# Half of the weight ring and half of the gated rows moved by 32 bytes: hash attention followed by a SwiGLU block

## The chip, the cores and the metric

The kernel runs on one core of a Trainium2 chip. The metric is the time on the device of one launch, in microseconds (us), median of the runs. A second number, the span, is the time from the first to the last instruction in one execution that was taken by the hardware profiler.

## The reference

Two blocks follow one another, all in float32.

```python
# attention with a hash mask: B, H, S, D = 4, 8, 768, 64; proj is 64 x 6
q_bucket = sum(((q @ proj) > 0) * powers);  k_bucket = the same of k
scores = where(q_bucket == k_bucket, q @ k.T / sqrt(D), -1e9)
attn_out = softmax(scores) @ v
# SwiGLU block: x is 3072 x 512, w_gate and w_val 512 x 1536, w_out 1536 x 512
x = attn_out as (B * S, H * D)
g = x @ w_gate
out = (silu(g) * (x @ w_val)) @ w_out
```

## The kernel before

**Two stages.** `attention` runs first, for 16 pairs of heads. Beside it the weights of the second block are turned into pieces of 128 x 3 x 512 float32 numbers and kept in DRAM (`ram`). A piece has three parts: high, low and the difference of the two. Rows of `x` are split into the same three parts. A product is then made of two sums of matmuls, one over the high and low parts (`a`) and one over the differences (`n`), and combined on the way out of PSUM. `gated_block` is the second stage, and the only one that the diff touches.

**Work of the second stage.** The 3072 tokens are three blocks of 1024. For each block there are 12 tasks U, numbered on through the blocks (n = 0 to 35), one for each 128 columns of the hidden dimension, and 4 tasks D (12 in all), each for three U. The list `order` (lines 219 to 225) writes the sequence out: U 0 to 3, D 0, U 4 to 6, D 1, and so on.

- A U makes two units, one for the gate and one for the value. A unit uses one ring place as the weights (the stationary operand) of 24 matmuls of 128 x 512: 16 into `a`, then 8 into `n` (`up`, lines 672 to 693). The moving operand is `xparts`: four tiles, j = 0 to 3, each with two halves of 512 tokens and three parts. For each half, `a` goes through j, and for each j through parts 0 and 1; `n` goes through j with part 2. ScalarE and VectorE then make the gated row tile `hid` from it, 128 x 3 x 1024 numbers (lines 709 to 726).
- A D goes through eight chunks of 128 tokens. Each chunk has nine matmuls (lines 738 to 754): for j = 0 to 2 the parts 0 and 1, then for j = 0 to 2 part 2. Here the weights are 128 columns of `hid` number 3 D + j, and the moving operand is a ring place with 512 columns. In the last D of a block the first four chunks begin with j = 0 and 1 alone. The sums go to `o` (lines 756 to 775), and after the fourth D of a block to DRAM.

**The weight ring.** The ring has six places. The first three, numbered 0 to 2, are in the pool `ringp`, made before the attention; the other three, 3 to 5, are in `late_ring`, made when the attention's buffers are given back. The list `wanted` (lines 226 to 231) holds the pieces in their order of use, and piece number i of it goes to place i mod 6 (`bring`, lines 234 to 244):

```python
pool = ringp[i % sum(RINGS) >= RINGS[0]]
held[what, n] = t = pool.tile([P, 3, PIECE], FP32R, tag="ring", name="ring")
nc.gpsimd.dma_start(t.bitcast(FP32), ram[at].bitcast(FP32))
```

Each unit asks for one more piece when its matmuls are written down, and each D for three. The loads go through the queue of GpSimd (POOL). The rows `hid` have four places, taken in turn.

**Where `xparts` lies** (`x_home`, lines 250 to 261). In block 0 all four tiles are in the pool `xparts`. In block 1, j = 0 and 1 are in the two buffers of the pool `stagep`, and j = 2 and 3 in `xparts`. In block 2, j = 0 and 1 are in `xparts`, and 2 and 3 in `stagep`.

**Addresses.** Pools lie one after another along each partition, in the order in which the code makes them (lines 69 to 76, then those of the stage), and a tile's room is rounded up to 32 bytes. All tile sizes of the second stage are multiples of 2048 bytes, as are the steps between the parts of a tile; the blocks of weights inside a part are 512 bytes apart. So whether a matmul's operand lies at a multiple of 64 bytes or 32 bytes past one is decided by the start of its tile. In the built program before, `stagep` begins at byte 28800 (offset 0 in 64), `xparts` at 53664 (offset 32), `ringp` at 105888 (32), `late_ring` at 124320 (32), `gatep` at 142752 (32), `hidp` at 159136 (32) and `outp` at 208288 (32).

Of the kernel before, what the change touches and what calls it, by code (L numbers as in the profile page):

```python
# [8 lines left out]
FP32 = mybir.dt.float32  # L9
FP32R = mybir.dt.float32r  # L10
# [9 lines left out]
def kernel(  # L20
# [24 lines left out]
    P = 128  # L45
# [12 lines left out]
    WB = 2 * PIECE  # L58
# [41 lines left out]
    n = 0  # L100
# [550 lines left out]


    def gated_block(scope):
        ringp.append(scope.enter_context(tc.tile_pool(name="late_ring", bufs=RINGS[1])))
        gatep = scope.enter_context(tc.tile_pool(name="gatep", bufs=2))
        hidp = scope.enter_context(tc.tile_pool(name="hidp", bufs=4))
        outp = scope.enter_context(tc.tile_pool(name="outp", bufs=1))
        homes.append(outp)
        pp = scope.enter_context(tc.tile_pool(name="pp", bufs=4, space=PSUM))
# [4 lines left out]
        hids = {}  # L664
# [33 lines left out]
        def atoms_of(kind, n):  # L698
            if kind == "U":
                b = n // NF  # L700
                hid = hids[n] = hidp.tile([P, 3, WB], FP32R, tag="hid", name="hid")
                h, l, d = (hid[:, i] for i in range(3))
                gate, val = (gatep.tile([P, WB], FP32, tag=name, name=name) for name in "gv")
                ops = {}
# [108 lines left out]
        for kind, n in order:  # L813
# [12 lines left out]
            for at, atom in enumerate(atoms_of(kind, n)):  # L826
                tail = atom()
                finish(tails)
                if tail:
                    tails.append(tail)  # L830
                if changing and kind == "U" and f >= NF - 2 and at:
                    splits.pop(0)()
                if changing and kind == "D" and f == NF // NQ - 1:
                    if at == 0:
                        more = [split_x(b + 1, pr) for pr in range(NP // 2, NP)]
                        for x in more:
                            x.pop(0)()
                    if at in (7, 10):
                        for x in more:
                            x.pop(0)()  # L840
                count[0] += 1
                if left and count[0] in (6, 14):
                    left.append(left.pop(0)())
                    left[:] = [f for f in left if f]
                for _ in range(((1, 2, 2, 2) if kind == "U" else (1, 2, 2) + (1,) * 9)[at]):
                    step = next(mine, None)
                    if step:
                        step()

    with ExitStack() as scope:  # L850
        gated_block(scope)
# [32 lines left out]
```

## Time and profile before

| what | us |
|---|---|
| median of 3 runs (923.06 to 925.82) | 923.29 |
| the profiled execution's own time | 927.82 |
| its span | 926.0 |
| busy in the span: TensorE (PE) / VectorE (DVE) / ScalarE (ACT) | 912.7 / 666.4 / 456.2 |
| start of the first matmul of the second stage | 325.43 |
| first matmul of blocks 1 and 2 | 522.12 / 721.66 |
| end of the last matmul | 921.36 |
| busy with the 1152 `a`, 576 `n` and 864 `o` matmuls | 277.0 / 144.3 / 198.7 |

The granted clock of TensorE is 0.998 of full speed over the span. In the page, a line such as "L670" is a line of the kernel. All matmuls of the second stage are written by one helper, `mm`, and so have the line 670; they are told apart by the tile that they write. PEld is the loading of weights into TensorE, which goes on beside matmuls. A matmul is recorded with its start and with an end that is modelled, and it is still in the pipeline when the next begins; so the time that a row of matmuls takes is read from starts. In the rows of a timeline the columns are the start and the length in us, the engine, the line, the operation with its tiles and shapes, and the number of instructions that are merged. In the waits they are the total in us, the number of times and the longest. In the view of one line, the three numbers are the shortest, median and longest duration in ns.

### The profile page before, as it was taken

What the parts mean: (1) busy time and instruction counts of PE and PEld (TensorE: products, weight loads), DVE (VectorE), ACT (ScalarE), POOL (GpSimd) and SP (SyncE); (2) the same over time, 40 slices, a digit from 0 to 9 for tenths busy, and PEclk for the clock granted to TensorE, in tenths of its full rate; (3) what the DMA queues carried; (4) which work ended last, traced back from release to release, by engine and by line L of the source; (5) the groups of instructions that cost most, each with busy time, mean ns of one, the idle gap of its engine ahead of it and who ended that gap; (6) DMA issues with size and microseconds to landing.
All of it is one profiled execution on the core that took longest, in us unless ns stands there. A gap on an engine that the chain in (4) does not pass through costs nothing.

```text
span 926.0 us, 12980 instructions
## 1 busy us (share of the span) xinstructions
PE 912.7 (99%) x4789; PEld 638.9 (69%) x4789; DVE 666.4 (72%) x768; ACT 456.2 (49%) x814; POOL 91.6 (10%) x182
## 2 busy tenths in 40 slices
PE   8999989999999999999999999999999999999997
PEld 3444544444444478888888788888887888888886
DVE  4889989889989858779786756464658754474746
ACT  6889868888888654452414133331313233313220
POOL 2011100001101111000100000101010100001000
PEclk9999999999999999999999999999999999999999
DMA  7678787767886599685756563434444642526232
GB/s 171 136 185 205 201 207 172 166 180 200 242 213 206 179 384 318 229 284 206 292 187 243 207 226 103 175 133 170 137 145 151 234 147 103 187 69 208 99 136 92
DMA packets 145296, 174.28 MB, mean 188 GB/s; under 512 B 106481, under 2 KB 114897, under 8 KB 145233
## 3 DMA queue, kind: packets, MB, share of 16 engines
q0 software_dynamic: 22528, 116.14, 36.0%
q1 hardware_dynamic: 121904, 57.12, 24.3%
q8 instruction: 38, 0.62, 0.3%
q10 hardware_dynamic: 800, 0.20, 0.1%
q14 instruction: 26, 0.20, 0.1%
HBM read 133.17 MB, written 39.42 MB: 186 GB/s over the span
## 4 chain that ended last, share of the span: by engine, by line
PE 95%; DVE 2%; DMA 1%; SPq 1%; issue 0%; ACT 0%; DVEq 0%; ACTq 0%; POOLq 0%
PE a L670 29%; PE o L670 19%; PE sc L504 16%; PE n L670 14%; PE av L518 14%; PE sum L557 1%; PE hps L436 1%; SPq L337 1%; DMA kraw<-in_k_dram 0%; DVE hid L725 0%; DVE v L715 0%; DVE hid L723 0%; DVE v L719 0%; DMA qb<-qb 0%; DMA proj<-in_proj_dram 0%
## 5 line engine op out<-in xcount | busy, mean ns | idle before, releaser
L670 PE MATMUL a<-xparts,ring 128*128 128x512 f32 x1152 | 277.0, 392 | 0.6 <-ACT row L560 0.6
L670 PEld LDWEIGHTS a<-xparts,ring 128*128 128x128 f32 x1152 | 216.2, 188 | 50.2 <-ACT row L560 1.3
L670 PE MATMUL o<-ring,hid 128*128 128x512 f32 x864 | 198.7, 390 | 1.1 <-DVE hid L725 1.1
L670 PEld LDWEIGHTS o<-ring,hid 128*128 128x128 f32 x864 | 161.9, 188 | 36.0 <-DVE hid L725 2.4
L507 ACT ACTIVATE A<-sc 128x384 f32<-128x384 f32 x384 | 157.3, 492 | 12.6 <-PE sc L504 12.6
L504 PE MATMUL sc<-qT,kT 64*128 64x384 f32 x768 | 158.9, 491 | 0.0
L670 PE MATMUL n<-xparts,ring 128*128 128x512 f32 x576 | 144.3, 393 | 0.0
L518 PE MATMUL av<-A,vraw 128*64 128x386 f32 (+1 forms) x768 | 127.7, 488 | 0.0
L670 PEld LDWEIGHTS n<-xparts,ring 128*128 128x128 f32 x576 | 108.1, 188 | 24.3
L715 DVE TENSOR_TENSOR v<-v,n 128x1024 f32<-128x1024 f32 x36 | 44.0, 1221 | 104.0 <-PE n L670 103.4
L244 POOL DMA_DIRECT2D ring<-ram x108 | 56.9, 529 | 506.9 <-PE n L670 334.9
L504 PEld LDWEIGHTS sc<-qT,kT 64*128 64x128 f32 x768 | 69.2, 189 | 51.3 <-issue 50.3
L518 PEld LDWEIGHTS av<-A,vraw 128*64 128x64 f32 x768 | 53.7, 136 | 73.3 <-issue 61.6
L709 ACT ACTIVATE g<-a 128x1024 f32<-128x1024 f32 x36 | 37.0, 1026 | 134.0 <-PE a L670 127.8
L720 ACT ACTIVATE hid<-v 128x1024 fp32r<-128x1024 f32 x36 | 38.2, 1061 | 115.9 <-DVE v L719 112.9
L717 ACT ACTIVATE g<-g 128x1024 f32<-128x1024 f32 x36 | 38.2, 1061 | 84.7 <-DVE g L715 84.7
L772 DVE TENSOR_TENSOR o<-o 128x512 f32<-128x512 f32 x92 | 63.0, 687 | 20.6 <-ACT o L766 18.2
L504 PE MATMUL sc<-qb,kb 64*128 64x384 bf16 x384 | 65.4, 325 | 3.4 <-DMA qb<-qb 2.9
L715 DVE TENSOR_TENSOR g<-g,n 128x1024 f32<-128x1024 f32 x36 | 43.8, 1216 | 34.2 <-PE n L670 34.2
L539 DVE SCALAR_TENSOR_TENSOR both<-A 128x1536 f32<-128x1536 f32 x32 | 55.9, 1748 | 13.6 <-ACT A L507 13.0
L543 DVE TENSOR_TENSOR both<-both,A 128x1536 f32<-128x1536 f32 x32 | 56.3, 1759 | 3.3
L723 DVE SCALAR_TENSOR_TENSOR hid<-hid,v 128x1024 fp32r<-128x1024 f32 x36 | 44.0, 1223 | 19.2 <-ACT hid L720 19.1
(76 smaller groups left out, 696.9 us busy)
## 6 DMA issues: line engine op xcount, KB each, us to landing
ring<-ram POOLq DMA_DIRECT2D x108, 768.0 KB, 5.1
ram<-stage POOLq DMA_DIRECT2D x23, 768.0 KB, 5.7
ram<-stage SPq DMA_DIRECT2D x13, 768.0 KB
qraw<-in_q_dram SPq DMA_DIRECT2D x64, 96.0 KB
vraw<-in_v_dram SPq DMA_DIRECT2D x16, 384.0 KB
out_dram<-o SPq DMA_DIRECT2D x24, 256.0 KB
kraw<-in_k_dram SPq DMA_DIRECT2D x62, 96.0 KB
r<-sums SPq DMA_DIRECT2D x30, 192.0 KB
```

Source lines behind the costliest of these rows:

```text
L244: nc.gpsimd.dma_start(t.bitcast(FP32), ram[at].bitcast(FP32))
L504: nc.tensor.matmul(sc[h], x["k", n][rows, ks], x["q", n][rows, qs], start=start, stop=not start)
L507: nc.scalar.activation(weights(u)[:, h, 0:HQ], sc[h], AF.Exp, scale=SCALE * (OFF / 2 if n == 0 else 1.0))
L518: nc.tensor.matmul(ps[h * D : (h + 1) * D, 0:width], raws["v", n][:, h, c, :], a[:, h, 0:width], start=c == 0, stop=c == NCH - 1)
L539: nc.vector.scalar_tensor_tensor(out=t, in0=first, scalar=S * EPS / P / 2, in1=now, op0=ALU.add, op1=ALU.add)
L543: nc.vector.tensor_tensor(t, t, now, op=ALU.add)
L670: nc.tensor.matmul(ps, w, x, start=start, stop=stop)
L715: nc.vector.tensor_tensor(two(z), two(z), n_, op=ALU.subtract)
L717: nc.scalar.activation(z, z, AF.Silu)
L720: nc.scalar.activation(h, val, AF.Copy, scale=TOWARD / STEP)
L723: nc.vector.scalar_tensor_tensor(out=l, in0=h.bitcast(FP32), scalar=-STEP, in1=val, op0=ALU.mult, op1=ALU.add)
L772: nc.vector.tensor_tensor(accs[c], accs[c], t[:, 1], op=ALU.subtract)
```

## The change

Three small tiles of 32 bytes per partition, which nothing reads or writes, are laid between the pools of the second stage, and the pool of the gated rows is made into two of two buffers each. In the built program `late_ring` begins at byte 124352 (offset 0 in 64), `gatep` at 142816 (32), the first two gated rows at 159200 (32), the other two at 183808 (0), and `outp` at 208384 (0). Gated rows with an even n take the buffers of the first pool and those with an odd n the buffers of the second; a buffer is used again after four, as before. The number of instructions and their order on each engine are the same.

```diff
     def gated_block(scope):
+        def shift(name):
+            scope.enter_context(tc.tile_pool(name=name, bufs=1)).tile([P, 8], FP32, tag=name, name=name)
+
+        shift("shift_ring")
         ringp.append(scope.enter_context(tc.tile_pool(name="late_ring", bufs=RINGS[1])))
+        shift("shift_gate")
         gatep = scope.enter_context(tc.tile_pool(name="gatep", bufs=2))
-        hidp = scope.enter_context(tc.tile_pool(name="hidp", bufs=4))
+        hidp = [scope.enter_context(tc.tile_pool(name="hidp", bufs=2))]
+        shift("shift_hid")
+        hidp.append(scope.enter_context(tc.tile_pool(name="more_hid", bufs=2)))
         outp = scope.enter_context(tc.tile_pool(name="outp", bufs=1))
...
-                hid = hids[n] = hidp.tile([P, 3, WB], FP32R, tag="hid", name="hid")
+                hid = hids[n] = hidp[n % 2].tile([P, 3, WB], FP32R, tag="hid", name="hid")
```

## The prediction

> **What bounds the kernel now.** I read the page first: busy times and the chain that ended last.
>
> ```profile
> PE 912.7 (99%) x4789; PEld 638.9 (69%) x4789; DVE 666.4 (72%) x768; ACT 456.2 (49%) x814; POOL 91.6 (10%) x182
> ...
> PE 95%; DVE 2%; DMA 1%; SPq 1%; issue 0%; ACT 0%; DVEq 0%; ACTq 0%; POOLq 0%
> PE a L670 29%; PE o L670 19%; PE sc L504 16%; PE n L670 14%; PE av L518 14%; PE sum L557 1%; PE hps L436 1%; SPq L337 1%; DMA kraw<-in_k_dram 0%; DVE hid L725 0%; DVE v L715 0%; DVE hid L723 0%; DVE v L719 0%; DMA qb<-qb 0%; DMA proj<-in_proj_dram 0%
> ```
>
> TensorE carries 95% of the chain, and 62% of the span is the matmuls of line 670, the gated block, which alone uses the buffers that move. Next, the waits of PE from 318 us to the end:
>
> ```profile
> PE o L670 <- DVE hid L725: 1.1, 3, 0.4
> PE a L670 <- ACT row L560: 0.6, 1, 0.6
> ```
>
> PE waits 1.7 us in 600. So the stage lasts as long as its 2592 matmuls, and the question is the time from one matmul's start to the next, the pitch. A matmul's own duration overlaps the next one, so I read starts, in the timeline of PE. Two units of the first token block, then two of the second (a unit is 16 `a` and 8 `n` matmuls on one ring place):
>
> ```profile
> 347.34 3.79 PE L670 MATMUL a<-xparts,ring 128*128 128x512 f32 x16
> 350.97 1.98 PE L670 MATMUL n<-xparts,ring 128*128 128x512 f32 x8
> 352.78 3.79 PE L670 MATMUL a<-xparts,ring 128*128 128x512 f32 x16
> ...
> 527.69 3.88 PE L670 MATMUL a<-xparts,ring 128*128 128x512 f32 x16
> 531.40 2.02 PE L670 MATMUL n<-xparts,ring 128*128 128x512 f32 x8
> 533.25 3.88 PE L670 MATMUL a<-xparts,ring 128*128 128x512 f32 x16
> ```
>
> From `a` to the next `a`: 352.78 - 347.34 = 5.44 us in block 0, 226.7 ns a matmul; 533.25 - 527.69 = 5.56 us in block 1, 231.7 ns. Same instructions, no idle time in either. The down projection, from the chain in order of time, one row in each block:
>
> ```profile
> 369.26 16.32 PE o L670 x72
> ...
> 566.82 16.32 PE o L670 x72
> ...
> 766.35 16.32 PE o L670 x72
> ```
>
> 16.32/72 = 226.7 ns in all three blocks. What differs between the two kinds of unit is where `xparts` lies. In block 0 all four home tiles are in the `xparts` pool, 32 bytes past a multiple of 64, as every ring place is. In blocks 1 and 2 two of the four are in the `stage` buffers, at a multiple of 64. Starts of single matmuls in the unit at 632.7 us show it: in `n` the pitches are 235, 235, 230, 227, then 234, 235, 231, 227 ns, for tiles j = 0 to 3, of which 0 and 1 are those in `stage`. In block 2 `stage` holds 2 and 3, and the slow ones swap with it. So a pair of matmuls whose moving operand lies at offset 0 while the weights lie at 32 loses 7.5 + 8.3 ns, and the next one 4.1. By the grouped line 670 in one unit of each kind:
>
> ```profile
> L670 PE MATMUL a<-xparts,ring x16: 389/389/389, 352.8 to 356.2; 128*128 128x512 f32 x16
> ...
> L670 PE MATMUL a<-xparts,ring x17: 389/395/397, 632.7 to 638.3; 128*128 128x512 f32 x17
> ```
>
> The excess over 226.67 ns, summed over starts, is 0.04 us in U of block 0, 3.04 in block 1, 3.02 in block 2, 0.13 in all D. That is 6.06 us for 576 matmuls at offset 0, 10.5 ns each with what spills into neighbours.
>
> **The Trainium skill.** "TensorE: Matmul & The Clock Gate", Step-by-step: what each phase is for, says PE has two independent SBUF read ports, so that loading the next weights takes nothing from the running matmul. The trace disagrees twice: 226.7 ns is above the 215.7 ns that the same page gives for back-to-back matmuls of 512 columns (Wait — 56ns, not 53.3ns?), and the pitch depends on where an operand lies. "SBUF — State Buffer", Operand start alignment, calls any multiple of the element size legal, and says its runs timed nothing. The same page (Door 1) tells of 16-byte lines; all operands here start on such a line, so it prices nothing.
>
> **The change part by part.** Order and count of instructions on every engine stay as they are; addresses move. Offsets in 64 bytes, before to after: ring places 0 to 2 stay at 32; places 3 to 5 go 32 to 0; gated rows of even n stay at 32, of odd n go 32 to 0; `g` and `v` stay at 32; `o` goes 32 to 0; `xparts` stays. I call a matmul mixed when its moving operand and its weights differ in this offset. Before: 576 mixed, 6.06 us.
>
> *U, block 0*: of 24 units 10 take their weights from places 3 to 5, now at 0, against `xparts` at 32: 240 mixed. Long runs cost less each than pairs; the second run of four in a slow unit alternates 7.5 and 5.7 ns, the first 7.5, 8.3, 5.0, 8.3, so 7 ns: 240 x 7 = 1.7 us.
>
> *U, blocks 1 and 2*: the 28 units with early places stay as they are. The 20 with late places have weights at 0: the tiles in `stage` now match, the other two are mixed. 12 of 24 before, 12 after: nothing, if mixed costs the same both ways round.
>
> *D* (moving: ring; weights: gated rows): before, none mixed. After, walking the ring order (places 2,3,4; 5,0,1; 2,3,4; 3,4,5 in each block) against odd and even n, just one of the three j in each D is mixed: 24 of 72 matmuls, in each chunk one pair (v = 0, 1) and one single (v = 2). Pair 19.9 ns as measured; single 7.5 + 4.1 = 11.6, an estimate from the same row: 8 x 31.5 = 0.25 us, times 12 = 3.0 us.
>
> *VectorE and ScalarE*: same kinds before and after; 1024-wide operations on `xparts` in `stage` take 1217 to 1226 ns as on the others. Even 10 ns on each would hide under PE: DVE works 384 us of the stage's 596. Uncovered, the last PE tail has two such operations: 0.02 us.
>
> *Waits*: the wait for the xT store that line 720 had at n = 0 (3.0 us, ACT idle, PE not) goes to n = 1, when the store has long landed. One PE wait in the first D moves two matmuls back. Ring loads keep their waits; they land in 5.1 us and are asked for five units (27 us) ahead. Nothing.
>
> Sum: 1.7 + 3.0 = 4.7 us for 528 more mixed matmuls; at 6.6 or 10.5 ns each it is 3.5 or 5.5. The profiled execution is 927.82 us (926.0 span, 1.8 around it), 4.5 above the median 923.29; its matmul pitches are repeated to the nanosecond in every unit, so I add the difference to the median.
>
> **Unknown prices.** Three pairings never occur before: moving 32 on weights 0, 0 on 0, and equal in 64 but 64 apart in 128 (all matching matmuls above are equal in 512). Below, streaming alone is 512/2.4 GHz = 213.3 ns, so a matmul could gain at most 13.3; above, the slowest seen is 236, a loss of 9. I take each by its offset in 64, since 0 against 32 is the only contrast that the trace has.
>
> **Rivals.**
> *Only the moving offset counts.* A moving operand at 0 is slow whatever the weights. For it: every slow matmul has one. Then U stays, and D has 576 such matmuls (ring places 3 to 5), in pairs and fours: at 19.9 ns a pair and 43 a four, 5.3 us. It can't be told by time from my sum; together they put the change at 4.7 to 5.3, and I take 4.9. Should the weights being loaded for the next matmul decide, D has 569 mixed and the sum is 6.9.
> *Finer than 64.* If only operands equal in 128 bytes run at 226.7, another 816 are slow: at about 7 ns in long runs the total is 14.6 against 6.06, +8.6 us, 931.9.
> *One direction only.* Weights at 32 under moving 0 is slow, the reverse free. Then mixed falls to 336 in U and rises by 216 in D: 5.8 against 6.06, 923.0; by next weights +1.2. Nothing in the trace speaks against it.
> *Faster: the new distance of 64 is better than 0.* 226.7 is 13.3 above streaming, so equal addresses may themselves collide. 816 matmuls get this distance. It decides when each gains over 4.7/816 = 5.8 ns; at 11 ns (down to the page's 215.7) -9.0 + 4.7 = -4.3, 919.0. Against it: all pitches of the trace but two, just after a start of PE, are 226 or more.
> *It does nothing*: `stage` is slow for its place, not its offset, and the time stays. Against it: `stage` ends at 53376 and the first fast `xparts` tile begins at 53664.
>
> **Numbers.** Mixed or moving offset counts (4.7 to 6.9): 0.62. Finer than 64: 0.10. One direction: 0.13. Nothing: 0.05. Faster: 0.10. The likeliest is 923.3 + 4.9 = 928.2, its own range 926.5 to 930.5. The range for 8 in 10 goes from 922.5 (one direction, nothing) to 932.5 (finer than 64) and leaves out the faster rival. About 0.3% (2.8 us) is what a measurement can tell; slower 0.72, same 0.18, faster 0.10.
>
> **What would show it.** Units of block 0 on late places at 5.6 us beside 5.44 on early ones; D at 16.57 us for 72; units of blocks 1 and 2 at 5.56. Moving only: block 0 all 5.44, D at 16.7 to 16.8. One direction: block 0 all 5.44 and late units of blocks 1 and 2 too. Wrong altogether: a pitch below 226, or new idle time of PE ahead of line 670.

## The result and the profile after

| | before | after |
|---|---|---|
| median of 3 runs, us | 923.29 (923.06 to 925.82) | 929.09 (928.66 to 931.45) |
| the profiled execution's own time / its span | 927.82 / 926.0 | 931.45 / 929.6 |
| second stage: start of its first matmul to end of its last | 325.43 to 921.36: 595.92 | 323.11 to 924.98: 601.88 |

The changed kernel is slower: the ratio is 1.0067, with a 95% interval of 1.0046 to 1.0087, and the medians are 5.8 us apart. The spans of the two profiled executions are only 3.6 us apart, because the first stage, which the change does not touch, took 2.3 us more in the execution before. There PE waited 2.9 us for a transfer of `qb`, against 2.1 after, and TensorE's granted clock was at half from 131.4 to 134.8 us, where it was full after. The second stage is 5.96 us longer, and that is the number that answers to the medians.

The groups of the page after, with the lines of TensorE (busy us, mean ns of one, then idle time before):

```profile
L677 PE MATMUL a<-xparts,ring 128*128 128x512 f32 x1152 | 278.1, 393 | 0.6 <-ACT row L560 0.6
...
L677 PE MATMUL o<-ring,hid 128*128 128x512 f32 x864 | 203.3, 395 | 0.7 <-DVE hid L732 0.7
...
L677 PE MATMUL n<-xparts,ring 128*128 128x512 f32 x576 | 144.8, 393 | 0.0
```

Line 670 is now 677. Against 277.0, 198.7 and 144.3 us before, most of the new time is in `o`, the matmuls of D. It is not idle time. The waits of PE in the second stage:

```profile
PE o L677 <- DVE hid L732: 0.7, 3, 0.3
PE a L677 <- ACT row L560: 0.6, 1, 0.6
```

They were 1.1 and 0.6 us before. The matmuls themselves follow one another more slowly. In the timeline of PE in block 0, the first two rows are units on early ring places, the next three on late ones, which the change moved (rows of `n` left out):

```profile
328.68 3.79 PE L677 MATMUL a<-xparts,ring 128*128 128x512 f32 x16
...
334.12 3.79 PE L677 MATMUL a<-xparts,ring 128*128 128x512 f32 x16
...
339.57 3.89 PE L677 MATMUL a<-xparts,ring 128*128 128x512 f32 x16
...
345.16 3.90 PE L677 MATMUL a<-xparts,ring 128*128 128x512 f32 x16
...
350.76 3.90 PE L677 MATMUL a<-xparts,ring 128*128 128x512 f32 x16
```

From start to start the units on early places take 5.44 and 5.45 us, as before, and those on late places 5.59 and 5.60. A D took 16.32 us before, in each of the nine that have no wait of PE in them. After, in the chain in order of time (start, us, what):

```profile
367.41 16.75 PE o L677 x72
...
417.29 16.68 PE o L677 x72
...
567.54 16.75 PE o L677 x72
```

Summed over the starts of single matmuls, the excess over 226.67 ns is now 12.49 us against 6.23 (both with D): U of block 0 has 1.68 (before 0.04), U of blocks 1 and 2 together 6.10 (6.06), D 4.71 (0.13). The place of the loss is the one that was forecast. What makes a matmul slow turned out to be another rule. The prediction also named a pitch below 226 ns as a sign of being wrong; there are 27 single ones of 224 or 225 ns after, each with slow pitches next to it, and no row that is faster than before.

### The profile page after: what moved, and what is told of

It is laid out like the page before. It is cut to its first block, busy times and chain, and to the rows that moved or that the text cites. A ratio compares the mean times of both kernels' runs of the same rounds, so it can differ in the third digit from the quotient of the medians.

```text
span 929.6 us, 12980 instructions
## 1 busy us (share of the span) xinstructions
PE 917.8 (99%) x4789; PEld 638.4 (69%) x4789; DVE 666.8 (72%) x768; ACT 456.7 (49%) x814; POOL 91.6 (10%) x182
## 4 chain that ended last, share of the span: by engine, by line
PE 91%; DVE 3%; SPq 3%; DMA 2%; ACT 1%; issue 1%; DVEq 0%; ACTq 0%
PE a L677 29%; PE o L677 20%; PE n L677 14%; PE sc L504 14%; PE av L518 11%; SPq L337 2%; PE sum L557 1%; PE hps L436 1%; DMA kraw<-in_k_dram 0%; PE idle L367 0%; DVE hid L732 0%; DVE hid L730 0%; DVE v L722 0%; DVE v L726 0%; DMA r<-sums 0%
## 5 line engine op out<-in xcount | busy, mean ns | idle before, releaser
L677 PE MATMUL o<-ring,hid 128*128 128x512 f32 x864 | 203.3, 395 | 0.7 <-DVE hid L732 0.7
L775 DVE SCALAR_TENSOR_TENSOR o<-o 128x512 f32<-128x512 f32 x72 | 49.4, 687 | 12.9 <-PE o L677 12.7
```

The lines of the kernel that those rows point to most:

```text
L677: nc.tensor.matmul(ps, w, x, start=start, stop=stop)
L775: nc.vector.scalar_tensor_tensor(out=accs[c], in0=t[:, 0], scalar=STEP + 1, in1=accs[c], op0=ALU.mult, op1=ALU.add)
```

## The experiments

In the following, the distance of a matmul is the address of its moving operand minus that of its weights, in bytes along the partition. Where a number under 256 is given for it, that is the remainder of a division by 256, which turned out to be what counts: 224 means 32 bytes short of a multiple. A matmul whose distance is not a multiple of 256 is called unequal. The theory at the start was the prediction's: a matmul is slow when its operands differ in the offset in 64 bytes ("mixed"). All kernels are made from the kernel before, except the last one; `shift` is the function of the change, which makes an unused tile, with its size as a last argument (32 bytes if none is given) and its pool as scope. All ratios are to runs of the kernel before on the same chip.

**One part alone: the ring.** The two unused tiles put the late ring places 32 bytes further, and the gated rows 64, which the theory takes for no move.

```diff
+        shift(scope, "shift_ring")
         ringp.append(scope.enter_context(tc.tile_pool(name="late_ring", bufs=RINGS[1])))
+        shift(scope, "shift_gate")
```

> Ring places 3 to 5 alone go to offset 0 in 64; all gated rows stay at 32. Theory (a matmul is slow when its moving operand and its weights differ in the offset in 64): U as in the changed kernel (late units of block 0 at 5.60 us, +1.7 us in all); in D the late places are the moving operand at 0 on weights at 32, 576 matmuls, +5.3 us, D at 16.6 to 16.9 us; +7 us in all, about 930.3. Rival (only the moving offset counts): U of block 0 all at 5.44 us, +5.3 us. Rival (it is the weights being loaded for the next matmul): no difference from the theory here, since all weights of a D lie at 32.

Measured: 929.18 us, ratio 1.0054 (1.0035 to 1.0074). U has the excess of the changed kernel, 7.82 us, with the late units of block 0 at 5.60. D lies at 16.69 to 16.76 us, within the forecast. So "only the moving offset counts" is out: the slow units of block 0 have the same `xparts` at the same place as before, and only their weights moved. For D the run is not a test of the ring alone: with the 64 bytes of the gated rows all 864 matmuls of D are unequal (distances 192 and 224), those on early places through that move only.

**The other part alone: the gated rows.**

```diff
-        hidp = scope.enter_context(tc.tile_pool(name="hidp", bufs=4))
+        hidp = [scope.enter_context(tc.tile_pool(name="hidp", bufs=2))]
+        shift(scope, "shift_hid")
+        hidp.append(scope.enter_context(tc.tile_pool(name="more_hid", bufs=2)))
...
-                hid = hids[n] = hidp.tile([P, 3, WB], FP32R, tag="hid", name="hid")
+                hid = hids[n] = hidp[n % 2].tile([P, 3, WB], FP32R, tag="hid", name="hid")
```

> Gated rows of odd n alone go to 0; the ring stays at 32. Theory: U exactly as before; D with 24 mixed matmuls (even D) at 16.6 us, with 48 (odd D) at 16.8 us; +4.4 us in all, about 927.7. By its own weights, the slow pitches are those of j with odd n; by the weights being loaded for the next matmul, those one place earlier. Rival (only the moving offset counts): nothing changes, 923.3.

Measured: 929.92 us, ratio 1.0062 (1.0041 to 1.0083). U is as before. D takes 16.80 us where 24 of its 72 matmuls are mixed and 16.75 where 48 are, so the forecast had the two the wrong way round, and the number of mixed matmuls is not what sets a D's time. Slow pitches begin one place earlier than the mixed matmuls: 226, 235, 231, 229, 234, 236 ns in the first D, where matmuls 3 and 4 are mixed. The two parts do not add up: the run with the ring lengthens the second stage by 6.0 us, the rows alone by 4.9, the change by 5.96. In D all three lose about the same: 4.87, 5.39 and 4.71 us of excess.

**Steps of 64 bytes.** Two of the changed kernel's three unused tiles, ahead of the late ring and ahead of the second pair of gated rows, with 64 bytes each; the one ahead of `gatep` is left out. The late places and the even gated rows thus go 64 bytes further, the odd ones 128.

```diff
+        shift(scope, "shift_ring", 16)
         ringp.append(scope.enter_context(tc.tile_pool(name="late_ring", bufs=RINGS[1])))
...
+        shift(scope, "shift_hid", 16)
+        hidp.append(scope.enter_context(tc.tile_pool(name="more_hid", bufs=2)))
```

> As the changed kernel, with steps of 64 bytes in place of 32: late ring places 64 further, gated rows of even n 64 and of odd n 128 further. Theory (offset in 64 alone counts): no pitch changes, D at 16.32 us, units of block 0 at 5.44, 923.3 us. Rival (finer: operands have to be equal in 128 or more): late units of block 0 and most of D slow, +5 to +9 us.

Measured: 929.24 us, ratio 1.0059 (1.0037 to 1.0081). Nothing differs in the offset in 64 except what did before, and the kernel loses as much as with 32. Its timeline in block 0, early place and then late ones:

```profile
334.97 3.79 PE L676 MATMUL a<-xparts,ring 128*128 128x512 f32 x16
...
340.41 3.90 PE L676 MATMUL a<-xparts,ring 128*128 128x512 f32 x16
...
346.01 3.90 PE L676 MATMUL a<-xparts,ring 128*128 128x512 f32 x16
```

340.41 to 346.01 is 5.60 us with the weights 64 bytes further than in the kernel before (distance 192), the same as with 32 (distance 224). With this the theory of the offset in 64 fell.

**Stage buffers 32 bytes further.**

```diff
+    shift(ctx, "shift_stage")
     stagep = ctx.enter_context(tc.tile_pool(name="stagep", bufs=2))
+    shift(ctx, "shift_small")
     small = ctx.enter_context(tc.tile_pool(name="small", bufs=3))
```

> The two stage buffers of the kernel before go 32 bytes further (offset 32), all else keeps its offset; so no matmul of the second stage is mixed. Theory: units of blocks 1 and 2 at 5.44 us in place of 5.56, 6.0 us less, about 917.3. Rival (the stage buffers are slow for their place, not for their offset): 923.3 and units at 5.56.

Measured: 922.52 us, ratio 0.9987 (0.9975 to 1.0000). It isn't the 917.3 of the theory. Units of blocks 1 and 2 take 5.55 us in place of 5.57: the distance of their slow half is now 192 in place of 224, and that is only a little cheaper.

**Everything at offset 0.**

```diff
+    shift(ctx, "shift_xparts")
     xparts_p = ctx.enter_context(tc.tile_pool(name="xparts", bufs=1))
...
+        shift(scope, "shift_att")
         opnd = scope.enter_context(tc.tile_pool(name="opnd", bufs=2))
```

> Every operand of line 670 at offset 0 in 64 (xparts, ring and gated rows moved to 0, the stage buffers stay there). Theory (equal offsets count): the same as with all at 32, units at 5.44 us in all blocks, D at 16.32, about 917.3. Rival (a moving operand at 0 is slow in itself): all 2592 matmuls slow at about 7 ns, +12 us, 935. Rival (weights at 0 touch 8 blocks of 64 bytes in place of 9): a pitch below 226.7, by up to 1.5 ns, 2 to 4 us less still.

Measured: 922.60 us, ratio 0.9989 (0.9980 to 0.9998), with the same pitches as the kernel at 32: U of block 0 at 5.44 us and D at 227.0 ns a matmul, with moving operand and weights both at 0. The theory's 917.3 was missed again, and by the same units of blocks 1 and 2, at 5.55. No row came out below 226.7 ns a matmul. So neither offset is good or bad in itself.

**All of U mixed, none of D.** The stage buffers as two runs above, and another 32 bytes ahead of `ringp`. As in the last run, 32 bytes ahead of `opnd` keep the attention's tiles at their offset in 64.

```diff
+    shift(ctx, "shift_ring")
     ringp = [ctx.enter_context(tc.tile_pool(name="ringp", bufs=RINGS[0]))]
...
+        shift(scope, "shift_att")
         opnd = scope.enter_context(tc.tile_pool(name="opnd", bufs=2))
```

> xparts all at 32, ring and gated rows all at 0: every matmul of U is mixed, none of D. Theory: units at 5.60 us in all blocks (1728 matmuls at 6.7 ns, 11.6 us, against 6.06 before), D at 16.32; +5.5 us, 928.8. Rival (only the moving offset counts): U at 5.44, D at 16.75 or more; 923.

Measured: 929.79 us, ratio 1.0067 (1.0049 to 1.0084). U takes 5.60 us in all three blocks and D 227.1 ns a matmul. 1728 matmuls at unequal distance have an excess of 11.26 us, 6.5 ns each. Size and place are as forecast.

**All of D mixed.** The stage buffers as in the run with all at 32, and the gated rows 32 bytes further.

```diff
+        shift(scope, "shift_hid")
         hidp = scope.enter_context(tc.tile_pool(name="hidp", bufs=4))
```

> All at 32 but the gated rows, which are all at 0: every matmul of D is mixed, none of U. Theory: U at 5.44 us in all blocks, D at 72 x 233.4 ns = 16.80 us, 864 matmuls at 6.7 ns, 5.8 us against 6.06 before: 923.0. It gives the price of a long mixed row in D beside the 16.67 to 16.75 us that the changed kernel's D take with only a third of the matmuls mixed by their own weights: if D lies below those, alternation costs more than being mixed throughout.

Measured: 926.96 us, ratio 1.0061 (1.0023 to 1.0099). One of the five executions took 935.5 us and widens the interval; the medians are 3.3 us apart. The second stage is 600.04 us, 4.1 more than before. The forecast of 923.0 missed, because it had taken U for cured, which keeps an excess of 5.19 us; the 5.8 us for D came true, with 5.62. A D in the chain in order of time:

```profile
364.28 16.80 PE o L676 x72
413.73 16.79 PE o L676 x72
463.17 16.80 PE o L676 x72
```

16.80 us for 72 matmuls is 6.5 ns each over 226.67. All D of the changed kernel lie just below it, though a third of their matmuls were thought to be mixed. So nearly all of them seem to pay, as the later rule has it. In this kernel the last `n` matmul ahead of a D has a pitch of 235 ns in all 8 cases where its own operands are at an equal distance; the first of the unequal weights are those of the matmul after it. The pitch rises one matmul early, in the time in which the next weights are loaded. Whether that load holds up the running matmul, or the next matmul starts late on its own account, no run separates.

**16 bytes.** The stage buffers as in the run with all at 32, and the ring places 16 bytes further in their room.

```diff
-            held[what, n] = t = pool.tile([P, 3, PIECE], FP32R, tag="ring", name="ring")
+            room = pool.tile([P, 3 * PIECE + 16], FP32R, tag="ring", name="ring")
+            held[what, n] = t = room[:, 4 : 3 * PIECE + 4].rearrange("p (v c) -> p v c", v=3)
```

> All at 32 but the ring places, which lie at 48: 16 bytes apart from the other operand in every matmul of line 670. If what counts is a grid of 32 bytes or coarser: pitches of 226.7 ns, 917.3. If any difference within 64 counts as much as 32 does: 2592 matmuls at 6.7 ns, 17.4 us on top of 917.3, 934.6. If the price grows with the distance: about half of that, 926.

Measured: 930.45 us, ratio 1.0074 (1.0059 to 1.0090). The larger rooms put the places 64 bytes apart from each other in 256, so the distances are 48, 112, 176 and 240 in U, and 16, 80, 144 and 208 in D. None of the three forecasts came true: 2592 unequal matmuls have 14.69 us of excess, 5.7 ns each, and the 917.3 us on which the forecasts build is not what the kernel with all at 32 takes (922.52). Nearly all units take 5.55 to 5.60 us, at each of the four distances, and D 16.6 to 16.8. So 16 bytes cost about as much as 32, with no growth with the distance.

Three units one after another, at 449.51, 454.95 and 460.39 us, are an exception that no rule of this document explains. The first two rows here are the gate unit of U 3 and the one after it; then come the gate unit of U 9 and the one after it:

```profile
354.67 3.90 PE L676 MATMUL a<-xparts,ring 128*128 128x512 f32 x16
...
360.27 3.90 PE L676 MATMUL a<-xparts,ring 128*128 128x512 f32 x16
```

```profile
454.95 3.79 PE L676 MATMUL a<-xparts,ring 128*128 128x512 f32 x16
...
460.39 3.79 PE L676 MATMUL a<-xparts,ring 128*128 128x512 f32 x16
```

Both gate units use ring place 0 on the same tiles of `xparts`, so their addresses are the same (distance 240). Yet the first takes 5.60 us and the second 5.44. All 72 matmuls of the three units run at 226.7 ns with unequal operands (distances 176, 240 and 176). In the other kernels no more than two unequal matmuls in a row have pitches of 228 ns or less. So an unequal distance is not slow every time; what sets these three units free is open.

By now every long row whose distance is a multiple of 512 had run at 226.7 ns, and, these three units apart, no row at 16, 32, 64 or 96 bytes from one. How large the period is was open.

**Two pools change places.** The pool `small` takes up 288 bytes, which is just what the stage buffers lack to be a multiple of 512 from the rest.

```diff
-    stagep = ctx.enter_context(tc.tile_pool(name="stagep", bufs=2))
     small = ctx.enter_context(tc.tile_pool(name="small", bufs=3))
+    stagep = ctx.enter_context(tc.tile_pool(name="stagep", bufs=2))
```

> The pools of stage buffers and of small tiles change places in the kernel before, which puts the two stage buffers 288 bytes further and nothing else; every moving operand of line 670 then lies a multiple of 512 bytes from its weights. New theory (a matmul runs at 226.7 ns only when its operands are a multiple of some larger power of two apart, 128 to 512 bytes, since 16, 32, 64 and 96 bytes all were slow): units of blocks 1 and 2 at 5.44 us in place of 5.56, 6.0 us less, about 917.5. If the stage buffers are slow for another reason: units at 5.56, 923.5.

Measured: 917.64 us, ratio 0.9932 (0.9916 to 0.9948), and the second stage is 589.80 us, 6.1 less than before. It beats both kernels. Its line 670, all 576 `n` matmuls by shortest, median and longest duration, and its timeline in block 1:

```profile
L670 PE MATMUL n<-xparts,ring x576: 389/389/389, 324.0 to 892.6; 128*128 128x512 f32 x192
```

```profile
527.73 3.79 PE L670 MATMUL a<-xparts,ring 128*128 128x512 f32 x16
531.36 1.98 PE L670 MATMUL n<-xparts,ring 128*128 128x512 f32 x8
533.17 3.79 PE L670 MATMUL a<-xparts,ring 128*128 128x512 f32 x16
```

533.17 - 527.73 is 5.44 us, in a block where it was 5.56. The excess of the whole stage is 0.10 us.

**128 and 256 bytes.** The last kernel, with 128 bytes after the stage buffers and 256 ahead of the gated rows; U of blocks 1 and 2 is half at a distance of 128, D all at 256.

```diff
+    shift(ctx, "shift_xparts", 32)
     xparts_p = ctx.enter_context(tc.tile_pool(name="xparts", bufs=1))
...
+        shift(scope, "shift_hid", 64)
         hidp = scope.enter_context(tc.tile_pool(name="hidp", bufs=4))
```

> As the run before, but with all later pools 128 bytes further than the stage buffers, and the gated rows another 256 further than the ring; so in blocks 1 and 2 half of the matmuls of U have operands 128 bytes apart (in 512), all of D 256 apart, and the rest are equal in 512. The new theory leaves the size open: with 128 enough, all pitches 226.7 ns, U at 5.44 us and D at 16.32; with 256 needed, units of blocks 1 and 2 near 5.56 and D at 16.32; with 512 needed, units near 5.56 and D at 16.7 to 16.8.

Measured, in a single execution of 922.57 us: D at 16.32 to 16.34 us, units of block 0 at 5.44, of blocks 1 and 2 at 5.54 to 5.55.

```profile
562.33 16.33 PE o L675 x72
```

```profile
578.50 3.85 PE L675 MATMUL a<-xparts,ring 128*128 128x512 f32 x16
584.04 3.86 PE L675 MATMUL a<-xparts,ring 128*128 128x512 f32 x16
```

A distance of 256 is free, one of 128 is not. The period is 256 bytes.

**The change itself with 256 bytes.** All lines of the changed kernel, and only the size of the three unused tiles differs.

```diff
-            scope.enter_context(tc.tile_pool(name=name, bufs=1)).tile([P, 8], FP32, tag=name, name=name)
+            scope.enter_context(tc.tile_pool(name=name, bufs=1)).tile([P, 64], FP32, tag=name, name=name)
```

> The changed kernel with its three small tiles made 256 bytes each in place of 32; all its other lines stay. If operands have to be a multiple of 256 bytes apart and nothing else of the change costs: every pitch as in the kernel before (units of block 0 at 5.44 us, of blocks 1 and 2 at 5.56, D at 16.32), no difference, 923.5. If the split of the gated rows or the moved waits cost something, that is what is left.

Measured: 923.48 us against 923.73, ratio 0.9996 (0.9985 to 1.0007); the second stage is 595.96 us against 595.92, and the D without a wait are as before:

```profile
563.52 16.32 PE o L677 x72
```

The split pool and the moved waits cost nothing. So the loss comes from steps of 32 bytes in place of 256, and from nothing else in the change. (`o` keeps its offset in 64 here, so its move to offset 0 is not tested by itself. PE waits less than before after the change, and the excess of 6.26 us in the pitches leaves nothing for `o` to explain.)

The pitches of all kernels in one table. The excess is that over 226.67 ns a matmul; pitches with a wait of PE in them are left out.

| kernel | unequal in U / D | excess in U / D, us | second stage, us |
|---|---|---|---|
| before | 576 / 0 | 6.10 / 0.13 | 595.92 |
| after | 1056 / 864 | 7.78 / 4.71 | 601.88 |
| ring (rows 64 further) | 1056 / 864 | 7.82 / 4.87 | 601.91 |
| rows alone | 576 / 432 | 6.20 / 5.39 | 600.84 |
| steps of 64 | 1056 / 648 | 8.07 / 3.95 | 601.34 |
| stage at 32 | 576 / 0 | 5.10 / 0.15 | 594.92 |
| all at 0 | 576 / 0 | 5.11 / 0.25 | 595.04 |
| U mixed | 1728 / 0 | 11.26 / 0.36 | 601.25 |
| D mixed | 576 / 864 | 5.19 / 5.62 | 600.04 |
| ring by 16 | 1728 / 864 | 9.71 / 4.98 | 603.98 |
| pools changed | 0 / 0 | 0.02 / 0.08 | 589.80 |
| 128 and 256 | 576 / 0 | 5.07 / 0.21 | 594.94 |
| change with 256 | 576 / 0 | 6.10 / 0.16 | 595.96 |

In each of these kernels U and D have an excess of more than 0.4 us only where they have unequal matmuls, but it isn't in proportion to their number. A row in which all are unequal costs 5.3 to 6.5 ns each (D of the change, U mixed), while a unit that is half unequal costs 0.10 to 0.13 us, 9 to 10.5 ns for each of its 12, nearly as much as one that is unequal throughout (0.12 to 0.16). With the rows alone, where half of D is unequal, it is 12 ns each.

## Why the prediction held, and where its steps failed

The time was 929.09 us; 928.2 was forecast, with 926.5 to 930.5 for the likeliest case. The sum was 4.7 us, or 4.9 with the rival that was merged with it, and the stage lost 5.96. So the place of the loss and its rough size were foreseen, by a rule that is wrong; that the time fell into the narrow range is in part luck, since in D two errors worked against each other.

*What bounds the kernel, and that a shift of 32 bytes can cost pitch.* Right. PE's waits went from 1.7 to 1.3 us, and the change with 256 bytes shows that moved waits and the split pool took nothing.

*U, block 0: 1.7 us.* Measured 1.68 against 0.04 before. The late units lie at 5.60 us as forecast, which holds under both rules, since they are at a distance of 224 throughout.

*U, blocks 1 and 2: nothing.* Measured 0.04 us more, but for another reason. The step said that late units have 12 mixed matmuls where they had 12 before. In truth all 24 are unequal (distances 192 and 224), and the number came out because a unit that is unequal throughout costs about as much as one that is half so: 5.57 us each.

*D: 3.0 us.* This is the step that failed most. It counted 24 of 72 matmuls as mixed, by the offset in 64, and put pairs and singles at their prices from U. In truth all 864 matmuls of D became unequal in 256, and they cost 4.71 - 0.13 = 4.58 us, 5.3 ns each. The step was short by 1.6 us. A D without a wait took 16.67 to 16.75 us where 16.57 was named as the sign of the theory. The error in the count (a third of the true one) was partly made good by a price that was too high for long rows (10.5 against 5.3 ns).

*The unknown prices.* The text took "equal in 64 but 64 apart in 128" as equal and said that the trace had no example of it. That was the assumption to distrust. It also noted that all matching operands were equal in 512. A period of 128, 256 or 512 was the other reading of the same trace.

*The rivals.* "Finer than 64" had the right kind of rule, with 128 for 256, and the right count, 1920 unequal matmuls; it forecast 14.6 us of excess, at about 7 ns for long rows, where 12.49 were measured, 6.5 each. "Only the moving offset counts" fell with the late units of block 0. "One direction only" fell with the same units, whose weights lie at 0 under a moving operand at 32. "The distance of 64 is better" fell with the steps of 64. "It does nothing, `stage` is slow for its place" fell with the two pools that changed places.

*What the Trainium skill said.* Its statement that loading the next weights steals no read bandwidth of SBUF, the memory of both operands, from the running matmul ("TensorE: Matmul & The Clock Gate", Step-by-step: what each phase is for) gives no reason for a price of addresses. Here the pitch depends on where the weights lie relative to the moving operand, by 6.5 ns of 226.7 in long rows. The prediction called this a disagreement; it is one only if the loads cause the loss, which no run shows. The 215.7 ns that the page gives for matmuls of 512 columns one after another (Wait — 56ns, not 53.3ns?) was seen at no distance; the best is 226.7. Why an equal distance is the cheapest, and what lies behind the 11 ns that remain, no run here tells.

## What to carry to other kernels

When matmuls follow one another without idle time, read the time from start to start, by tile, and look for one kind of operand that is slow in every block: a difference of 2% between two kinds of the same instruction is a fact to explain. On this kernel it was the distance of the two operands in 256 bytes, and changing the order of two pools, at no cost in memory, took 6.1 us out of the second stage. A rule that is read from one contrast should be tried at the other distances that it allows before it is used to count. And a run that moves one buffer moves those behind it too: count the distances of all pairs before calling it one part alone.

## What was not expected of the hardware

The time from one 128 x 512 float32 matmul with new weights to the next is 226.7 ns in rows in which moving operand and weights lie a multiple of 256 bytes apart along the partition. At each of the other distances that occurred, it is 231 to 234 ns on average: 16, 48, 80, 112, 128, 144, 160, 176, 192, 208, 224 and 240. None was faster than equality. Three units in the run with 16 bytes, at distances of 176 and 240, ran at 226.7 ns all the same, so equality was always enough here, but not always needed. The pitches of rows with unequal matmuls mostly come back in the same pattern in unit after unit, between 224 and 241 ns, and slow ones reach past the last unequal matmul, by one to four in the kernel before; within its unit at 632.7 us they run 230, 236, 228, 233 over four matmuls whose own operands are equal.
